# Gate and up stage: a weight load moved to mid block, and row sums moved from the first to the second block of each pair

## The chip, the core and the metric

The kernel runs on one core of a Trainium2 chip. Times are device microseconds (us). The time before is 1020.63 us, the median of three runs (1020.56 to 1021.0). The profile comes from a further execution.

A core has five engines that work side by side, each through its own instructions in order. The profile calls them PE (TensorE, the matrix products; PEld is its loading of the weights), DVE (VectorE), ACT (ScalarE), POOL (GpSimd) and SP (SyncE, which here only issues DMA transfers; its rows read SPq).

## What is computed

The reference mixes two branches of the same input x (2048 rows by 640 columns) with a gate for each row:

```python
g = sigmoid((x * gate_w).sum(-1, keepdims=True))
a = dft_seq_re @ (x @ dft_hid_re.T) - dft_seq_im @ (x @ dft_hid_im.T)
b = (gelu(x @ w_gate) * (x @ w_up)) @ w_down
out = g * a + (1 - g) * b
```

All inputs are float32. w_gate and w_up are 640 by 1728, w_down is 1728 by 640.

## The kernel before, in words

**Products.** Each float32 operand is split into a high part (rounded to the type float32r, on ACT: `high`, line 81) and a low part, the rest (on DVE: `low`, line 84). One product is three matmuls, high by high, high by low and low by high (`mm3`, lines 99 to 103, so PE rows carry the lines L101, L102, L103). Tile names end in h and l for the two parts and in r for the raw data. The products are put together from two by two blocks in a scheme that needs seven block products in place of eight, at the price of sums of blocks on DVE. The names A11, A12, A22, S1 to S4 stand for weight blocks and their sums, T1 to T4 for the sums of the right hand side.

**Stages.** First comes a short stage with the narrow columns, then the gate and up stage (blocks f = 1 to 12, lines 1178 to 1260, some 46 to 334 us of the profile), then the product with w_down, the product along the sequence and the product along the hidden dimension.

**The gate and up stage.** Block f computes 128 columns of x @ w_gate and x @ w_up, for two halves of the rows (tp = 0 and 1), with `gate_up` (line 501). From f = 3 on the blocks come in pairs. `pair_of(f)` gives 1 for the first block of a pair (3, 5, 7, 9, 11, some 30 us each) and 2 for the second (4, 6, 8, 10, 12, some 18 us each). A first block also runs `together` (line 428, banks H, Z, V with the ending t) and `together_up` (line 468, banks with the ending u), which do one product of the pair over both halves of the rows. `together_up` needs weights made from `load_up` (tile wu..r, lines 227 to 232), by `make_up` (line 241: `across`, then the high parts, then `low_u`), and the tiles xu, which POOL loads back from DRAM with `load_across` (line 1148) three times in each first block from f = 5 on. In the same way POOL loads three tiles xq for `together` toward the end of the second block ahead of it.

**What sets the order.** While a block's products are traced, a list `fills` of small pieces of work for the other engines is worked off. Each piece has a cost in ns; `fill` (line 1155) takes pieces from the front as PE's work advances, and never two costless ones in a row after another piece. So a piece's place in `fills` is its place in the program, and `in_order` (line 108) holds PE, ACT, DVE and POOL to the program's order in this stage. SP isn't held: its transfers are placed by the compiler's scheduler, and start when the slot of their tile is free.

The pieces that the change touches:

- `make_w(f + 1)` (line 264) makes the weights of the next block: their sums on DVE, high parts on ACT, low parts on DVE or, in a first block's weights, by a negated copy on ACT and an accumulating transfer on POOL (`left_of`, line 95). Its list is `work`, lines 367 to 378.
- `sum_wd(k)` (line 606) prepares weights of the last product, that with w_down: `load` fetches the tiles dr (512 KB, line 612) and da (128 KB), and two pieces `do` of two DVE sums each (lines 595, 596, 599, 600) form block sums, which SP stores to wsd (line 602). Before, `load` is called at the top of each first block, and the two sums stand behind `make_up`.
- `load_z(n)` (line 709) serves the gate's logits: `load` fetches a tile xz of x (320 KB, line 716), and `total` (line 720) multiplies it by gate_w and adds up each row, on DVE. Sixteen such tiles are needed, ten of them in this stage. Before, two go into each of the blocks 5, 7, 9 and 11, and one into 6 and 8 (`ZE_AT`).

**Slots.** Most tiles, raw, high or low, share 46 equal slots of 4 KB in each partition (`slot`, line 72). A tile that finds none free waits until an earlier tile's last reader is done: the DMA issue or the engine that writes it first waits. Small tiles (da, wb) and half tiles have pools of their own.

Of the kernel before, what the change touches and what calls it, by code (L numbers as in the profile page):

```python
# [22 lines left out]
NF = F // P  # L23
# [4 lines left out]
EORD = [0, 2, 1, 3, 4]  # L28
PAIRED = 3
ZB_AT = [5,7,9,14,15,16]  # L30
ZE_AT = [6, 8]
XB_DOWN = [17, 18]
XB_AT = [1, 3, 4, 5, 9, 10]
WU_AT = [4, 17, 19, 33, 35]
# [3 lines left out]
def kernel(  # L38
# [33 lines left out]
    def slot(dt, shape, name):  # L72
        return pool.tile(shape, dt, tag="s4", name=name, bufs=46)
# [33 lines left out]
    @contextmanager  # L107
    def in_order(*engines):

        traced = nc.cur_bb.bb.instructions  # L110
        mark = traced[-1]
        yield
        start = next(k for k in reversed(range(len(traced))) if traced[k] is mark) + 1
        dep = mybir.DependencyInfo(mybir.DependencyClass.NoSync, mybir.DependencyReason.DATA)
        prev = {}
        for ins in traced[start:]:
            if ins.engine in engines:
                if ins.engine in prev:
                    tc.add_manual_dep(ins, prev[ins.engine].name, dep, reason="in_order")
                prev[ins.engine] = ins  # L120
# [21 lines left out]
    def at(hilo, i):  # L142
        h, l = hilo
        return h[:, i], l[:, i]
# [60 lines left out]
    def pair_of(f):  # L205


        return 0 if f < PAIRED or f >= NF else 2 - (f - PAIRED + 1) % 2
# [18 lines left out]
    def load_up(f):  # L227

        r = slot(F32, [P, 8, P], f"wu{f}r")
        nc.sync.dma_start(r[:, 0:2], wf[f, :, 2:4])  # L230
        nc.sync.dma_start(r[:, 6:8], wf[f - 1, :, 2:4])
        return r
# [8 lines left out]
    def make_up(f, r):  # L241

        W, own = {}, {}

        def across():
            tt(r[:, 2], r[:, 0], r[:, 1], op=ALU.add)
            tt(r[:, 4], r[:, 6], r[:, 0], op=ALU.subtract)
            tt(r[:, 3], r[:, 2], r[:, 6], op=ALU.subtract)
            tt(r[:, 5], r[:, 7], r[:, 3], op=ALU.subtract)

        def high_u():
            own["u"] = [slot(F32R, [P, 8, P], f"wu{f}{n}") for n in "hl"]
            high(own["u"][0][:, 1:6], r[:, 1:6])

        def low_u():
            u = own["u"]
            low(u[0][:, 1:6], u[1][:, 1:6], r[:, 1:6])
            W["A22p"] = at(u, 1)
            for k in range(4):
                W[f"S{k + 1}p"] = at(u, 2 + k)  # L260

        return W, [(112, across), (0, high_u), (78, low_u)]
# [343 lines left out]
    def sum_wd(k):  # L606

        work = []

        def load():  # L610
            r, a21 = slot(F32, [P, 8, P], f"dr{k}"), wsmall(F32, f"da{k}")
            nc.sync.dma_start(r, wd[k, :, :8])
            nc.sync.dma_start(a21, wd[k, :, 8:])
            work.extend(do for _, do in sums_left(nc.sync, r[:, 0:2], r[:, 2:4], r[:, 6:8], a21, wsd[k]))

        def do():
            work.pop(0)()

        return [(0, load), (84, do), (84, do)]
# [89 lines left out]
    def load_z(n):  # L709

        r, work = {}, []

        def load():
            sb = zq.pop(0)
            r[0] = sb, slot(F32, [P, D], f"xz{sb}")
            nc.sync.dma_start(r[0][1], xz[sb])

        def total():
            sb, v = r.pop(0)
            nc.vector.tensor_tensor_reduce(v, v, gwb, 1.0, 0.0, ALU.mult, ALU.add, z[:, sb : sb + 1])  # L720

        return [(0, load), (80, total)] * n
# [99 lines left out]
    def split_pieces(i):  # L822

        n = "{}{}{}".format(*kseq[i])
        r, raw = kraw.pop(i)
        names = ("A11", "A12", "e5", "S4")
        assert not kseq[i][1]
        B, W = [], {}

        def weights():  # L830
            h, l = slot(F32R, [P, 8, P], f"kh{n}"), slot(F32R, [P, 8, P], f"kl{n}")
            split(h, l, r)
            W.update({name: (at((h, l), 2 * q), at((h, l), 2 * q + 1)) for q, name in enumerate(names)})

        def right(q):
            v = hl(f"kb{n}{q}")
            split(*v, raw[q])
            B.extend([at(v, 0), at(v, 1)])

        ktile[i] = W, B  # L840
        return [(122, weights), (122, lambda: right(0)), (122, lambda: right(1))]
# [177 lines left out]
    with in_order(ACT, DVE, PE):  # L1019
# [5 lines left out]
        for d in range(ND):  # L1025
# [20 lines left out]
            if d == 0:  # L1046
                wh, wl = W0["m"][0]
                for c in halves:
                    for k, (w, x) in enumerate(((wh, h), (wl, h), (wh, l))):
                        first = k == 0 and c is halves[0]  # L1050
# [33 lines left out]
        W, work = make_w(1)  # L1084
# [68 lines left out]
    fills, state = deque(), {}  # L1153
# [15 lines left out]
            fill(ns)  # L1169
            next(steps)  # L1170

    s1t, s4 = {}, {}
    Tp.update(B11=at(Bs[0][2, 1], 0), B21=at(Bs[0][2, 1], 1), B22=at(Bs[1][2, 1], 1))
    blocks = [("11", xt[0, 2]), ("12", xt[2, 2]), ("22", xt[2, 3]), ("21", xt[0, 3])]
    keptp, loadp, t123, t4 = sums_across("xp", Tp, blocks, lambda: at(Bs[1][2, 1], 0))
# [2 lines left out]
    with in_order(PE, ACT, DVE, POOL):  # L1178
        for f in range(1, NF):
            kind = pair_of(f)  # L1180
            if f == PAIRED:
                loadu()
                fills.extend([*t4, *u123[:3], *late_work, *u123[3:], *u4])
            fills.extend(todo)
            todo.clear()
            if kind == 1:
                up, work = make_up(f, load_up(f))
                fills.extend(work)
            if kind == 1:
                lw, *w = sum_wd((f - PAIRED) // 2)  # L1190
                lw[1]()
                fills.extend(w)
            if f == PAIRED - 1:
                loadp()
                fills.extend(t123)
            if f == NF - 1:
                lw, *w = sum_wd(NK - 1)
                lw[1]()
                fills.extend(w)
            if f + 1 < NF:  # L1200
                nxt, work = make_w(f + 1)
                if kind != 1 or f == PAIRED:
                    fills.extend(work)
            if kind == 1 and f > PAIRED:
                (_, first), z1, (_, second), z2 = load_z(2)
                first()
                k = len(fills) // 2
                more = list(fills)
                fills.clear()
                fills.extend([*more[:k], z1, (0, second), *more[k:], z2, *work])  # L1210
            elif f in ZE_AT:
                (_, first), z1 = load_z(1)
                first()
                fills.insert(5, z1)
            if f == NF - 1:
                load_k(0)
                fills.extend(split_pieces(0))
                gates(0)
                nc.scalar.activation(table, table, AF.Gelu_apprx_tanh)
            state.update(pe=0, done=0, all=sum(c for c, _ in fills), pe_all=2450 if not kind else 2994 if kind == 1 else 1768)  # L1220
            s5 = pair(F32, f"s5{f}")
            xs = {}
            work = [gate_up(f, W, Bs[tp], tp, s5[:, tp], s1t, xs, s4) for tp in range(2)]
            more = together(f, W, Tp, s1t, xs) if kind == 1 else iter(())
            more_up = together_up(f, W, up, s4) if kind == 1 else iter(())
            store_left()
            if f in LEFT_AT:
                left_work.extend(LEFT_AT[f]())
                if f in (2, 12):
                    k = len(fills) // (2 if f == 2 else 1)  # L1230
                    rest = [fills.pop() for _ in range(len(fills) - k)]
                    fills.extend([*left_work, *reversed(rest)])
                    state["all"] = sum(c for c, _ in fills)
                    left_work.clear()
            for _ in range(4):
                run(more)
            for step in range(8 if not kind else 7):
                for tp, w in enumerate(work):
                    run(w)
                    if (step, tp) in ((0, 1), (1, 1)):  # L1240
                        run(more)
                        if step == 0:
                            run(more)
                    if (2, 0) < (step, tp) < (6, 0):
                        run(more_up)
                if step < 2 and kind == 1 and f > PAIRED:
                    for k in ((1,), (2, 3))[step]:
                        load_across(f, "xu", Tu, keptu, k)
                if step == 4 and pair_of(f + 1) == 1 and f + 1 > PAIRED:
                    for k in (1, 2, 3):  # L1250
                        load_across(f + 1, "xq", Tp, keptp, k)
                if step == 5:
                    load_w(f + 2)
                if f == NF - 1 and step > 4:
                    load_k(step - 4)
            for v in (more, more_up):
                next(v, None)
            while fills:
                fills.popleft()[1]()
            W = nxt  # L1260
# [438 lines left out]
```

## Time and profile before

| | |
|---|---|
| median of three runs | 1020.63 us |
| the profiled execution, in all | 1021.83 us |
| its span, first to last instruction | 1020.0 us |
| instructions | 13269, of them 4483 matmuls |
| DMA | 267.58 MB, mean 262 GB/s |
| mean granted TensorE clock | 1.000 |

How to read the rows that follow. In a timeline a row has the start in us from the span's start, the duration, the engine, the line, the operation, the tile written, `<-` and the tiles read, the shape, and in brackets the idle time of the engine ahead of it with what ended it as inferred. "x2" means two instructions merged into the row. In the rows of windows there follow, after the stretch and its length, the busy us of each engine with its instructions in parentheses in the order PE, PEld, DVE, ACT, POOL, then the granted clock, the DMA engines' busy share and GB/s. Rows of DMA issues end with the count, the size of one and the median us from issue to landing. "DMA to landing" rows give least, median and most for one tile. A matmul's end is modelled and overlaps the next one's start, so distances between starts tell more than durations.

### The profile page before, as it was taken

To read this page: it belongs to the slowest core of one execution; us is meant where nothing else is said; L and a number is where in the kernel's file an instruction comes from. 1 tells how busy PE (TensorE), PEld (TensorE's weight loads), DVE (VectorE), ACT (ScalarE), POOL (GpSimd) and SP (SyncE) were. 2 spreads that over 40 slices of the span, in tenths; PEclk is the share of its full clock that TensorE was granted. 3 is DMA by queue.
4 is the path that set the end of the run, shared out by engine and by line. 5 is a ranking of instruction groups with operands and counts; after the bars stand their busy time and mean duration, and the time that the engine had idled before them with its cause. 6 is when DMAs were issued, how large, how long until landed. Compare 5 with 4: busy or idle time off the path is not lost.

```text
span 1020.0 us, 13269 instructions
## 1 busy us (share of the span) xinstructions
PE 1015.6 (100%) x4483; PEld 840.2 (82%) x4483; DVE 823.2 (81%) x1154; ACT 486.1 (48%) x622; POOL 166.9 (16%) x295
## 2 busy tenths in 40 slices
PE   9999999999999999999999999999999999999998
PEld 7888888888888888888888888888888888888887
DVE  6987877787787989888887976898588869797796
ACT  5544534353535667557444443444344444455440
POOL 0122242323231200100001012102210200021112
PEclk9999999999999999999999999999999999999999
DMA  7468588968699999979874669668866877897856
GB/s 271 168 209 276 181 264 275 314 225 290 201 315 313 415 374 383 330 245 329 295 254 172 213 223 337 223 200 298 302 203 209 294 252 275 295 349 215 274 134 99
DMA packets 96644, 267.58 MB, mean 262 GB/s; under 512 B 12672, under 2 KB 27008, under 8 KB 96576
## 3 DMA queue, kind: packets, MB, share of 16 engines
q1 hardware_dynamic: 70512, 185.24, 53.2%
q0 software_dynamic: 25776, 81.30, 24.4%
q8 instruction: 35, 0.57, 0.2%
q14 instruction: 33, 0.27, 0.1%
q10 hardware_dynamic: 288, 0.20, 0.1%
HBM read 192.48 MB, written 70.27 MB: 258 GB/s over the span
## 4 chain that ended last, share of the span: by engine, by line
PE 97%; issue 1%; DMA 1%; DVE 0%; POOL 0%; POOLq 0%
PE pX L103 6%; PE pX L102 6%; PE pX L101 6%; PE pZ L103 4%; PE pZ L102 4%; PE pZ L101 4%; PE pL L102 3%; PE pL L103 3%; PE pL L101 3%; PE pV L102 2%; PE pV L103 2%; PE pV L101 2%; PE pY L102 1%; PE pR L103 1%; PE pQ L101 1%; PE pQ L102 1%
## 5 line engine op out<-in xcount | busy, mean ns | idle before, releaser
L82 ACT ACTIVATE ch<-csa 128x1024 fp32r<-128x1024 f32 x32 | 34.0, 1063 | 78.2 <-DVE csa L770 76.7
L85 DVE TENSOR_TENSOR cl<-cra,ch 128x1024 fp32r<-128x1024 f32 x32 | 39.1, 1222 | 24.6 <-ACT ch L82 22.5
L82 ACT ACTIVATE ch<-cra 128x1024 fp32r<-128x1024 f32 x32 | 33.9, 1059 | 52.3 <-DVE cl L85 19.3
L85 DVE TENSOR_TENSOR cl<-crb,ch 128x1024 fp32r<-128x1024 f32 x32 | 39.1, 1223 | 14.4 <-ACT ch L82 14.4
L102 PE MATMUL pL<-cl,xah 128*128 128x512 f32 x128 | 49.9, 390 | 0.0
L103 PE MATMUL pL<-ch,xal 128*128 128x512 f32 x128 | 49.9, 390 | 0.0
L101 PE MATMUL pL<-ch,xah 128*128 128x512 f32 x128 | 49.7, 390 | 0.0
L82 ACT ACTIVATE ch<-crb 128x1024 fp32r<-128x1024 f32 x32 | 33.8, 1055 | 31.2 <-PE pL L102 11.4
L404 POOL DMA_DIRECT2D hA<-s x48 | 26.1, 544 | 132.7 <-DVE s L562 113.1
L85 DVE TENSOR_TENSOR cl<-csb,ch 128x1024 fp32r<-128x1024 f32 x32 | 39.2, 1225 | 3.7 <-ACT ch L82 2.3
L85 DVE TENSOR_TENSOR cl<-csa,ch 128x1024 fp32r<-128x1024 f32 x32 | 39.1, 1221 | 2.1 <-ACT ch L82 1.1
L82 ACT ACTIVATE ch<-csb 128x1024 fp32r<-128x1024 f32 x32 | 34.0, 1062 | 11.7 <-DVE csb L773 4.7
L556 ACT ACTIVATE s<-s 128x512 f32<-128x512 f32 x24 | 15.2, 633 | 46.7 <-DVE s L555 46.7
L148 ACT ACTIVATE s<-pX 128x512 f32<-128x512 f32 x40 | 23.5, 598 | 23.7 <-PE pX L103 22.4
L85 DVE TENSOR_TENSOR kl<-kw,kh 128x1024 fp32r<-128x1024 f32 x24 | 29.4, 1223 | 4.5 <-DMA kw<-in_wd 2.6
L82 ACT ACTIVATE kh<-kw 128x1024 fp32r<-128x1024 f32 x24 | 25.3, 1052 | 16.1 <-PE kR L103 6.2
L551 DVE TENSOR_TENSOR s<-s,pX 128x512 f32<-128x512 f32 x24 | 16.5, 686 | 19.6 <-PE pX L103 14.3
L1346 POOL DMA_DIRECT2D uA<-c x8 | 4.3, 542 | 168.9 <-DVE c L1448 168.7
L404 POOL DMA_DIRECT2D hT<-s x48 | 26.0, 541 | 24.3 <-DVE s L579 8.1
L929 POOL DMA_DIRECT2D out<-ks x12 | 6.5, 541 | 136.8 <-DVE ks L928 136.2
L101 PEld LDWEIGHTS pL<-ch,xah 128*128 128x128 f32 x128 | 24.0, 188 | 5.0
L102 PEld LDWEIGHTS pL<-cl,xah 128*128 128x128 f32 x128 | 24.0, 188 | 5.0
(3612 smaller groups left out, 3483.8 us busy)
## 6 DMA issues: line engine op xcount, KB each, us to landing
cra<-in_ct SPq DMA_DIRECT2D x64, 512.0 KB, 4.6
crb<-in_ct SPq DMA_DIRECT2D x64, 512.0 KB, 5.0
hA<-s POOLq DMA_DIRECT2D x48, 256.0 KB, 5.9
hT<-s POOLq DMA_DIRECT2D x48, 256.0 KB, 5.7
kr<-hA SPq DMA_DIRECT2D x24, 512.0 KB, 7.7
kr<-hT SPq DMA_DIRECT2D x24, 512.0 KB, 6.8
ux<-uA SPq DMA_DIRECT2D x24, 512.0 KB, 5.9
ux<-uT SPq DMA_DIRECT2D x16, 512.0 KB, 6.7
```

Source lines behind the costliest of these rows:

```text
L82: nc.scalar.activation(hi, raw, AF.Copy)
L85: nc.vector.tensor_tensor(lo, raw, hi.bitcast(F32), op=ALU.subtract)
L101: nc.tensor.matmul(ps, lh, rh, start=first, stop=False, skip_group_check=True)
L102: nc.tensor.matmul(ps, lh, rl, start=False, stop=False, skip_group_check=True)
L103: nc.tensor.matmul(ps, ll, rh, start=False, stop=last, skip_group_check=True)
L148: nc.scalar.activation(m, src, AF.Copy)
L404: nc.gpsimd.dma_start(to[:, i], src)
L551: tt(s5, s5, X, op=ALU.add)
L556: nc.scalar.activation(s2, s2, AF.Gelu_apprx_tanh)
L929: nc.gpsimd.dma_start(acc4[:, t] if tp and e == 4 else out[2 * tp + t, e], src)
L1346: nc.gpsimd.dma_start(to[:, i], src)
```

## The change

Three things move, all in the loop of the gate and up stage:

1. In the first blocks from f = 5 on, `load` of `sum_wd` (`lw`) becomes a piece of `fills` behind the three pieces of `make_up`, ahead of the pieces of the next block's weights. The two DVE sums go behind the fifth of those pieces, the low parts of the next block's A weights. Block 3 keeps its order.
2. No piece of `load_z` stands in first blocks any longer, except that the blocks 7 and 9 fetch one tile as their last piece; its row sum is kept in `zlate` and goes into the next block, at position 4 of its list.
3. The second blocks 4, 6, 8 and 10 fetch two tiles each at their top, with the row sums at positions 9 and 12 of the list.

So the row sums lie 2, 2, 3, 3 in the blocks 4, 6, 8, 10, where they lay 2, 1, 2, 1, 2, 2 in 5, 6, 7, 8, 9, 11.

```diff
-ZE_AT = [6, 8]
+ZE_AT = (7, 9)
...
-    s1t, s4 = {}, {}
+    s1t, s4, zlate = {}, {}, []
...
             if kind == 1:
                 lw, *w = sum_wd((f - PAIRED) // 2)
-                lw[1]()
-                fills.extend(w)
+                if f == PAIRED:
+                    lw[1]()
+                    fills.extend(w)
...
             if kind == 1 and f > PAIRED:
-                (_, first), z1, (_, second), z2 = load_z(2)
-                first()
-                k = len(fills) // 2
-                more = list(fills)
-                fills.clear()
-                fills.extend([*more[:k], z1, (0, second), *more[k:], z2, *work])
-            elif f in ZE_AT:
-                (_, first), z1 = load_z(1)
-                first()
-                fills.insert(5, z1)
+                fills.extend([lw, *work[:5], *w, *work[5:]])
+                if f in ZE_AT:
+                    fetch, z1 = load_z(1)
+                    fills.append(fetch)
+                    zlate.append(z1)
+            elif kind == 2 and f < NF - 1:
+                if zlate:
+                    fills.insert(4, zlate.pop())
+                for k in (9, 12):
+                    (_, do), z1 = load_z(1)
+                    do()
+                    fills.insert(k, z1)
```

## The prediction, made before the changed kernel ran

> **What bounds the kernel now.** I read the page's busy table first, then the span (1020.0 us) cut into five stretches, of which three are shown.
>
> ```profile
> PE 1015.6 (100%) x4483; PEld 840.2 (82%) x4483; DVE 823.2 (81%) x1154; ACT 486.1 (48%) x622; POOL 166.9 (16%) x295
> ```
> ```profile
> 20.00:200.00 180.00, 180.00 (x794) 148.82 (x794) 146.36 (x246) 84.12 (x131) 45.77 (x82) 1.00 0.70 233
> 200.00:220.00 20.00, 19.88 (x88) 15.97 (x87) 13.97 (x29) 8.73 (x15) 2.47 (x5) 1.00 0.81 275
> 220.00:1000.00 780.00, 780.00 (x3442) 646.22 (x3441) 638.37 (x840) 379.34 (x452) 114.99 (x201) 1.00 0.80 272
> ```
>
> TensorE is busy for the whole span, at granted clock 1.00. A busy PE hides short gaps, because a matmul's shown time (0.39 us) is longer than the distance to the next one; so I count starts. From 220 to 1000 there are 3442 matmuls in 780 us, 226.6 ns each; from 20 to 200, 794 in 180 us, 226.7 ns each. That is one pitch throughout. Only 200:220 falls below its full length (19.88), and its PEld share is lower too (15.97 in 20 us, against 148.82 in 180 us, which is 16.54 in 20). The one gap lies here, in the timeline of PE and the chain of waits:
>
> ```profile
> 212.50 0.39 PE L103 MATMUL pX<-xT03h,ws7l 128*128 128x512 f32 x1
> 213.01 0.50 PE L101 MATMUL pH7u<-xu,wu7h 128*128 128x512 f32 x1
> 213.34 0.40 PE L102 MATMUL pH7u<-xu,wu7h 128*128 128x512 f32 x1
> ```
> ```profile
> 207.69 5.28 DMA xu<-xv
> ```
>
> The three starts are 0.51 and 0.33 us apart where 0.227 is the pitch: 0.28 + 0.10, and 0.01 in the next, **0.39 us lost**, in block 7 of the gate and up stage. PE waited for xu (the second tile of the block's up sums), whose load POOL issued at 207.69. Why so late, VectorE, POOL and SP tell:
>
> ```profile
> 197.88 0.68 DVE L585 TENSOR_TENSOR s<-s,s 128x512 f32<-128x512 f32 x1
> 202.20 0.83 DVE L720 CUSTOM_DVE_ANT_0 xz<-xz,gwb 128x640 f32<-128x640 f32 x1 [3.64 <-DMA hT<-s]
> ...
> 206.46 0.82 DVE L85 TENSOR_TENSOR wu7l<-wu7r,wu7h 128x640 fp32r<-128x640 f32 x1 [0.57 <-DMA hT<-s]
> ...
> 208.57 0.42 DVE L600 TENSOR_TENSOR dr<-dr 128x256 f32<-128x256 f32 x1
> ```
> ```profile
> 202.58 0.55 POOL L1150 DMA_DIRECT2D xu<-xv  x1 [0.30 <-issue]
> 207.69 1.14 POOL L1150 DMA_DIRECT2D xu<-xv  x2 [4.56 <-DVE dr L595]
> ```
> ```profile
> 191.04 0.62 SPq L612 DMA_DIRECT2D dr<-in_wd  x1
> 192.44 0.33 SPq L716 DMA_DIRECT2D xz<-in_xz  x1
> ```
> ```profile
> DMA to landing us min/median/max: 8.7/9.2/9.6
> ```
> ```profile
> xu<-xv POOLq DMA_DIRECT2D x12, 512.0 KB, 5.6
> xz<-in_xz SPq DMA_DIRECT2D x10, 320.0 KB, 7.8
> dr<-in_wd SPq DMA_DIRECT2D x5, 512.0 KB, 7.2
> ```
>
> (The three transfers are from the DMA list of this stage, 95 to 340: KB each, median us to landing.) VectorE stood 3.64 us at the logits' product L720. The wait's row names an hT store, but L720 reads only xz and gwb; the row of landings (8.7/9.2/9.6) is that of block 7's two xz tiles, and a load issued at 192.44 that takes 9.6 us lands at 202.0, just ahead of L720; so I read it as the xz landing. Behind it in VectorE's order stand the up-weights' sums and wu7l, the last reader of wu7r. POOL's xu loads start 0.41 us after wu7l ends (207.28), which fits a wait for wu7r's slot; the row blames the instruction behind it, L595.
>
> **The change part by part.** No instruction is added or dropped: ten L720 products, ten xz loads and the same dr loads, placed elsewhere. The matmuls stay 4483 at the same pitch, so the time can change only by PE's gaps, and 0.39 us is all that can be won after the first 20 us.
>
> *The logits' products leave the first blocks* (5, 7, 9, 11: two each before, none after). In block 7 VectorE gets back 3.64 + some 0.8 = 4.4 us ahead of wu7l, since its work before L720 ends at 198.6 (L585). So wu7l should end near 207.3 - 4.4 = 202.9, and the xu loads, two issues from about 203.3 on (behind the block's first xu load at 202.6), should land by 203.9 + 5.6 = 209.5. PE wants them at 212.73 (212.50 plus one pitch). **The 0.39 us go**, and 3 us are to spare. What is late next in that block is dr, below.
>
> *They enter the second blocks* (two in 4 and 6, three in 8 and 10). Against before that is +2, +1, +2, +3 products of 0.8 us: 1.6, 0.8, 1.6 and 2.4 us on VectorE. The cover is the idle time of VectorE ahead of the first product S3 or of wd in each of these blocks:
>
> ```profile
> 136.98 0.29 DVE L85 TENSOR_TENSOR wd<-wb,wd 128x128 fp32r<-128x128 f32 x1 [3.31 <-ACT wd L82]
> ...
> 185.68 0.69 DVE L551 TENSOR_TENSOR s<-s,pX 128x512 f32<-128x512 f32 x1 [1.65 <-ACT s L547]
> ...
> 233.81 0.69 DVE L551 TENSOR_TENSOR s<-s,pX 128x512 f32<-128x512 f32 x1 [3.58 <-ACT s L547]
> ...
> 280.47 0.29 DVE L85 TENSOR_TENSOR wd<-wb,wd 128x128 fp32r<-128x128 f32 x1 [3.31 <-ACT wd L82]
> ```
>
> 3.31, 1.65, 3.58 and 3.31 us cover 1.6, 0.8, 1.6 and 2.4: cost 0. Without that cover each would cost its own length at most, 6.4 us together. One product is not covered: in blocks 8 and 10 the one fetched in the block before goes in ahead of the second sums across (position 4), so wq, its accumulate on POOL and the xq load behind it slide by 0.8 us.
>
> ```profile
> 283.43 1.24 POOL L1150 DMA_DIRECT2D xq<-xp  x2 [3.35 <-DMA wq11l<-wq11r]
> ```
> ```profile
> 290.08 0.39 PE L101 MATMUL pH11t<-xq,wq11h 128*128 128x512 f32 x1
> ```
> ```profile
> DMA to landing us min/median/max: 4.1/4.9/6.7
> ```
>
> The last row is for the three xq of block 10. There 283.43 + 0.8 + 4.9 = 289.1, 1.0 us ahead of PE; at the longest landing 290.9, 0.8 late. For block 8 I take the same bounds: 0 and 1.6 us together. I take 0, the median of the landings being the row that fits the two tiles in question.
>
> *The xz loads move with them.* Two are issued at the top of each second block, a third at the end of blocks 7 and 9 behind dr and its stores on SP. They leave a stretch (190 to 205) in which block 7's first half had dr, xz and the hA and hT stores at once. The landing of 7.8 us must now fit between the block's top and the positions 9 and 12 of its list; see the second rival.
>
> *dr is loaded behind wu's low parts* instead of at the block's top, its two sums go behind low_a of the next block's weights. VectorE now waits for dr, with both S3 sums (L551), the next sums' low parts (low_c), L490 and both S4 sums (L555) queued behind, and PE waits for L490. If dr is issued only when wu7r's slot comes free, at 202.9, it lands at 210.1; its four sums take 1.7 us (from wu7l's end at 207.28 to L600's at 208.99), so they end at 211.8. The first S3 product behind them ends only at 212.9 (its last matmul, 212.50 + 0.39): cost 0, by 1.1 us. If SP gets an older slot, it is earlier still.
>
> The Trainium skill, "DMA: Bandwidth & Descriptors", section "Rules for kernel authors", says the opposite of this edit: issue the transfer early, compute, wait late. The same page's section "Anatomy of one DMA" gives 2.0 us plus bytes over 436 GB/s, an estimate of 3.2 us for dr's 512 KB. By that figure dr would land at 206.1 and no cost could arise; the row (7.2 us) says otherwise, and the sum goes by the row.
>
> **Sum.** 1020.0 of span - 0.4 = 1019.6 for the profiled execution. That execution took 1021.83 us in all, 1.20 above the median of the three runs; so I subtract the 0.4 from the median: 1020.63 - 0.39 = **1020.2 us**.
>
> **The rivals.** *It doesn't do what it says.* The xu loads wait for some other slot than wu7r's and stay late, or the gap stays at 0.2 to 0.6 us: 1020.4 to 1020.8, say 1020.6. For it speaks that the slot's owner is only inferred; against it, that the timing fits wu7l to 0.41 us. Chance 0.12.
>
> *The late xq* (above): 1020.2 + 0 to 1.6, up to 1021.8. Chance 0.09.
>
> *Slower: dr's slot passes on late.* Now the high parts of block 8's sums wait for dr's four stores, in the slot that dr leaves:
>
> ```profile
> 215.09 1.06 ACT L82 ACTIVATE ws8h<-ws8r 128x1024 fp32r<-128x1024 f32 x1 [0.48 <-DMA wsd<-dr]
> ```
> ```profile
> 217.32 0.68 DVE L490 TENSOR_TENSOR s<-s,pH7u 128x512 f32<-128x512 f32 x1
> ```
> ```profile
> 219.26 0.39 PE L101 MATMUL pH7u<-xT14h,wu7h 128*128 128x512 f32 x1
> ```
>
> From ws8h's start to the end of L490 it is 2.9 us (218.0 - 215.09), and pH7u would be due at 218.87 without the 0.39. The release came 6.1 us after the last sum (209.0 to 215.1). With the sums ending at 211.8 it comes at 217.9, L490 ends at 220.8, and PE loses 1.9 us, in each of blocks 5, 7, 9, 11 where the slots fall that way: 1022.1 with one, 1028 with four. It decides once the last sum ends after 218.87 - 2.9 - 6.1 = 209.9, that is, if dr lands after 208.2. For it speaks that the forecast's own dr lands at 210.1 when it takes wu7r's slot. Against it: the first half of the block holds two xz tiles less, so older slots are free for ws8h, or for dr itself. Chance 0.13. This is where the rule of the Trainium skill on issuing early would come out right.
>
> *Slower: the third xz lands late.* In blocks 8 and 10 three tiles need slots. In block 8 the first S3 sum must end by the first row's start:
>
> ```profile
> 237.62 0.39 PE L101 MATMUL pX<-x05h,wa 128*128 128x512 f32 x1
> ```
> ```profile
> 226.02 0.54 POOL L404 DMA_DIRECT2D hT<-s  x1 [0.18 <-issue]
> ```
> ```profile
> hT<-s POOLq DMA_DIRECT2D x48, 256.0 KB, 5.7
> ```
>
> L720, the sum behind it and S3's take 0.8 + 0.2 + 0.7, so the tile must land by 235.9 and be issued by 228.1. Slots of block 7's weights come free with its last matmuls, some 2 us behind 219.26, which is in time. If the tile got that of s, freed by the last hT store of that block (226.02 + 5.7 = 231.7), it would land at 239.5: 3.6 us in each of two blocks, 1027. Chance 0.07.
>
> **How the numbers follow.** The forecast, 1020.2, has 0.58; its own spread is that of the three runs, 1020.0 to 1020.8. 0.2% is 2.04 us, about what a measurement of this kernel can tell from no change. Faster by that is five times the gap that the starts show: 0.01. The two slower rivals hold 0.20, of which some 0.02 (one block alone) stays within 2 us: slower 0.18, within 0.2% either way 0.81. The range goes from 1019.8 to 1022.6, through the late xq and the dr rival in one block, and leaves out about 0.17.
>
> **What would show it.** Right: no L720 between 190 and 221, wu7l ending near 203, the second xu load issued near 203, every PE start of block 7 0.227 apart, xq ahead of 290.08 in block 10. Wrong: PE gaps at the last pH.u of the blocks 5, 7, 9, 11 with ws.h released by a wsd store; gaps at the last pX of block 8 or 10 with VectorE waiting at L720; or PE starts off the pitch in the later stages, which this change should not touch.

## The result, and the profile after

The changed kernel takes 1022.53 us (median of 20 executions, 1021.55 to 1029.86), the kernel before, on the same chip, 1021.05 us (20 executions, 1020.45 to 1022.62). The ratio is 1.0022, with a 95% interval of 1.0014 to 1.0030: 1.5 us slower, where 0.4 us faster was forecast. Of the 2.3 us between the forecast of 1020.2 and the result, 0.4 lie in the kernel before, whose median was 1020.63 in three executions and 1021.05 in twenty. The profiled execution took 1022.97 us with a span of 1021.2 us, 1.2 us more than that of before.

The stretches 20 to 200, 200 to 220 and 220 to 1000 again, now of the changed kernel:

```profile
20.00:200.00 180.00, 180.00 (x794) 148.74 (x794) 148.04 (x253) 84.70 (x131) 46.47 (x83) 1.00 0.71 235
200.00:220.00 20.00, 20.00 (x90) 16.49 (x89) 11.56 (x21) 9.76 (x16) 1.86 (x4) 1.00 0.71 236
220.00:1000.00 780.00, 778.45 (x3434) 644.32 (x3433) 637.76 (x840) 379.42 (x452) 114.58 (x200) 1.00 0.80 272
```

Two things are to be seen. 200:220 is full (20.00 with 90 matmuls, 88 before): the gap of block 7 is gone. And 220:1000, full before with 3442 matmuls, now lacks 1.55 us and holds 3434, eight matmuls fewer. The waits of PE name the place, and the timeline of PE shows it:

```profile
PE pH11t L101 <- DMA xq<-xp: 1.6, 1, 1.6
```
```profile
285.98 0.39 PE L101 MATMUL pH11t<-x021h,wa11h 128*128 128x512 f32 x1
...
289.15 0.39 PE L103 MATMUL pV11t<-x05h,wa11l 128*128 128x512 f32 x1
291.09 0.50 PE L101 MATMUL pH11t<-xq,wq11h 128*128 128x512 f32 x1 [1.55 <-DMA xq<-xp]
291.43 0.39 PE L102 MATMUL pH11t<-xq,wq11h 128*128 128x512 f32 x1
```

The starts are 1.94 and 0.34 us apart where 0.227 is the pitch: 1.71 + 0.11 = 1.8 us lost in block 11, on the second of the three xq tiles. Won 0.4, lost 1.8. How xq became late stands in the rows of VectorE, ACT and POOL in block 10 of the changed kernel:

```profile
273.73 0.68 DVE L525 TENSOR_TENSOR s<-s,pX 128x512 f32<-128x512 f32 x1
274.33 0.82 DVE L720 CUSTOM_DVE_ANT_0 xz<-xz,gwb 128x640 f32<-128x640 f32 x1
275.08 0.08 DVE L720 DVE_READ_ACCUMULATOR2_ANT z<- 128x1 f32 x1
275.08 0.28 DVE L291 TENSOR_TENSOR wq11r<-wa11r,wq11r 128x128 f32<-128x128 f32 x1
```
```profile
275.60 0.96 ACT L82 ACTIVATE wq11h<-wq11r 128x896 fp32r<-128x896 f32 x1 [1.74 <-DVE wq11r L292]
```
```profile
278.31 0.86 POOL L97 DMA_DIRECT2D wq11l<-wq11r  x1 [3.67 <-DMA wa11l<-wa11r]
279.13 0.60 POOL L1150 DMA_DIRECT2D xq<-xp  x1
284.95 0.56 POOL L1150 DMA_DIRECT2D xq<-xp  x1 [5.22 <-DMA wq11l<-wq11r]
```

The kept row sum (274.33 to 275.08) stands ahead of L291 and L292, and ACT waits for L292; wq's accumulating transfer follows, and the second xq load waits for that transfer to land, which frees wq11r's slot (by the row's releaser). The rows of the kernel before for the accumulate and for the first matmul of block 11:

```profile
278.24 0.86 POOL L97 DMA_DIRECT2D wq11l<-wq11r  x1 [2.92 <-ACT wq11l L93]
```
```profile
286.66 0.39 PE L101 MATMUL pH11t<-x021h,wa11h 128*128 128x512 f32 x1
```

Measured from that matmul (285.98 in the changed kernel, 286.66 before), the accumulate is issued 7.67 us ahead (8.42 before): the 0.75 us of the row sum. The changed kernel's row names the landing of wa11l as what ended POOL's wait. That is a coincidence: in two kernels below, e3_z_only and e8_wa_behind, wa11l lands later (7.49 and 7.40 us ahead) and the accumulate is still issued 7.67 us ahead, and in all four it follows the end of ACT's negated copy (L93) by 0.4 us. The second xq is issued 1.03 us ahead (3.23 before): 2.2 us later. These rows give the difference, first the landing of wq11l, then that of the second xq:

```profile
DMA to landing us min/median/max: 6.2/6.2/6.2
```
```profile
DMA to landing us min/median/max: 6.1/6.1/6.1
```

Before, the same two rows read 4.8 and 4.1. So a slip of 0.75 us grew by 1.4 us in the first landing and by 2.0 in the second: 4.2 us in all. The tile landed 5.07 us behind the block's start in place of 0.87, and PE wants it at 3.40.

The same slip in block 8 cost nothing. There the accumulate was issued 7.67 us ahead of block 9 too, landed in 4.6 us (4.1 before), and the second xq was issued 2.66 us ahead (3.92 before), landed in 3.6 us and was 2.5 us in time.

### The profile page after: what moved, and what is told of

Its sections match the earlier page's. It is cut to its first block, busy times and chain, and to the rows that moved or that the text cites. A ratio compares the mean times of both kernels' runs of the same rounds, so it can differ in the third digit from the quotient of the medians.

```text
span 1021.2 us, 13283 instructions
## 1 busy us (share of the span) xinstructions
PE 1015.3 (99%) x4483; PEld 840.0 (82%) x4483; DVE 823.3 (81%) x1154; ACT 487.7 (48%) x622; POOL 167.2 (16%) x295
## 4 chain that ended last, share of the span: by engine, by line
PE 94%; issue 3%; DMA 1%; POOL 1%; DVE 0%; POOLq 0%
PE pX L101 6%; PE pX L103 6%; PE pX L102 6%; PE pZ L101 4%; PE pZ L103 4%; PE pZ L102 4%; PE pL L103 3%; PE pL L101 3%; PE pL L102 3%; PE pV L103 2%; PE pV L101 2%; PE pV L102 2%; PE pY L103 1%; PE pR L103 1%; PE pQ L103 1%
## 5 line engine op out<-in xcount | busy, mean ns | idle before, releaser
L537 ACT ACTIVATE s<-pZ 128x512 f32<-128x512 f32 x24 | 14.2, 595 | 30.2 <-PE pZ L103 29.2
```

The costliest lines, as they stand in the source:

```text
L537: nc.scalar.activation(s5, Z, AF.Copy)
```

## The experiments

**Theory A**: VectorE's 0.75 us ahead of the second sums across does it, by way of wq's accumulate and crowded transfers. **Rival B**: the third xz tile of the blocks 8 and 10 crowds the transfers. **Rival C**: what costs is dr's later load. All twelve are read in one table. The first two columns are PE's loss by starts: from the first matmul of block 7 to that of block 9 beyond 47.68 us, and from the first of block 11 to PE's last beyond 729.52 us (the distances in profiles without a gap). The 0.45 of before are the prediction's 0.39 and small excesses in the matmuls behind. The last two belong to the second xq for block 11, measured from that block's first matmul: issue, and landing (wanted at 3.40; landings are read to 0.1 us).

| kernel | block 7 | block 11 on | median us (n) | ratio, 95% | issue | landing |
|---|---|---|---|---|---|---|
| before | 0.45 | 0.0 | 1021.05 (20) | | -3.23 | 0.87 |
| changed | 0.0 | 1.87 | 1022.53 (20) | 1.0014 to 1.0030 | -1.03 | 5.07 |
| e1_late5 | 0.0 | 0.0 | 1021.00 (11) | 0.9991 to 1.0009 | -3.23 | 1.67 |
| e2_no_third | 0.99 | 0.0 | 1021.42 (11) | 0.9999 to 1.0016 | -3.24 | 0.96 |
| e3_z_only | 0.0 | 0.0 | 1022.21 (11) | 1.0004 to 1.0023 | -1.78 | 2.92 |
| e4_dr_only | 1.87 | 0.0 | 1021.82 (11) | 1.0001 to 1.0019 | -3.23 | 1.87 |
| e5_before_delay | 0.05 | 0.12 | 1022.32 (11) | 0.9999 to 1.0016 | -1.76 | 3.34 |
| e6_after_delay2 | 0.60 | 0.34 | 1022.81 (12) | 1.0012 to 1.0034 | -5.80 | 1.60 |
| e7_late5_z | 0.0 | 0.0 | 1020.93 (12) | 0.9992 to 1.0011 | -3.21 | 1.99 |
| e8_wa_behind | 0.0 | 1.56 | 1021.99 (11) | 0.9996 to 1.0013 | -1.58 | 2.02 |
| e9_after_again | 0.75 | 0.94 | 1022.17 (1) | | -1.14 | 3.96 |
| e10_wa12_behind | 1.94 | 1.82 | 1022.91 (12) | 1.0002 to 1.0024 | -1.30 | 2.80 |
| e11_dr_not5 | 0.0 | 0.0 | 1021.13 (11) | 0.9991 to 1.0008 | -3.23 | 0.77 |
| e12_z_behind_up | 1.79 | 0.0 | 1021.91 (12) | 1.0000 to 1.0021 | -3.22 | 2.08 |

The ratios are to the kernel before, run on the same chip with each set: 1021.1 with e1 to e4, 1021.3 with e5 to e8, 1021.16 with e9 to e11, 1021.26 with e12.

### The first set: which part of the change

e1_late5 puts the kept row sum one place later, behind the second sums across:

```diff
-                    fills.insert(4, zlate.pop())
+                    fills.insert(5, zlate.pop())
```

> The kept row sum of blocks 8 and 10 goes one place further back, behind the second sums across; all else as changed. Theory A (the 0.75 us that VectorE adds ahead of the second sums across push wq's accumulate into the first xq load and the second xq load behind wa12r): PE's gap in block 11 (1.7 us) goes, time 1.2 to 1.8 us under the changed kernel, 1020.2 to 1020.8. Theory B (three xz tiles in a second block crowd the DMA engines and the slots, wherever VectorE uses them): the gap stays at 1.3 us or more. Theory C (dr loaded later is what costs): no difference from the changed kernel.

e2_no_third fetches no third tile; the two row sums it leaves over go into the last stretch of blocks, as elsewhere in the kernel:

```diff
-ZE_AT = (7, 9)
-ZB_AT = [5,7,9,14,15,16]
+ZE_AT = ()
+ZB_AT = [5, 7, 9, 11, 13, 14, 15, 16]
```

> Blocks 7 and 9 fetch no xz tile, so blocks 8 and 10 have two each; the two tiles left over are done in the product with w_down, at its steps 11 and 13. Theories A and B: the gap in block 11 goes, 1020.2 to 1020.8 unless the two steps of the later stage lose something of their own. Theory C: it stays, 1022 to 1022.6.

e3_z_only moves the row sums alone, e4_dr_only dr alone (in the first blocks from 5 on). Both edits are shown against the changed kernel, cut to what matters:

```diff
-                if f == PAIRED:
-                    lw[1]()
-                    fills.extend(w)
+                lw[1]()
+                fills.extend(w)
...
-                fills.extend([lw, *work[:5], *w, *work[5:]])
+                fills.extend(work)
```
```diff
-ZE_AT = (7, 9)
+ZE_AT = [6, 8]
...
-                fills.extend([lw, *work[:5], *w, *work[5:]])
...
+                (_, first), z1, (_, second), z2 = load_z(2)
+                first()
+                more = list(fills)
+                fills.clear()
+                fills.extend([*more[:4], z1, (0, second), *more[4:], lw, z2, *work[:5], *w, *work[5:]])
```

> The xz tiles and their row sums are placed as in the changed kernel, dr is loaded at the block's top with its sums behind the up-weights, as before. Theories A and B: the gap in block 11 stays (1 to 2 us), time 1021.5 to 1022.6. Theory C: no gap, 1020.2 to 1020.8.

> dr is loaded mid block and its sums stand behind low_a as in the changed kernel, the xz tiles and their row sums stand where they stood before. Theories A and B: no gap in block 11; the 0.4 us in block 7 may stay, since the row sum again waits ahead of wu7l: 1020.4 to 1021.0. Theory C: 1.7 us in block 11 or the like elsewhere, 1022 to 1022.6.

One place later is all it takes: 1021.0 us, no gap, three tiles as in the changed kernel. B falls with that. e1_late5 also has dr moved in every block as the changed kernel has it, so C alone does not explain the changed kernel's loss. e2_no_third, which B and A both allow, loses nothing in block 11, as A needs, but 0.99 us in block 7, so its time (1021.42) missed the forecast. The POOL rows of e1_late5 carry it:

```profile
277.51 0.86 POOL L97 DMA_DIRECT2D wq11l<-wq11r  x1 [2.92 <-DVE ws11r L282]
279.20 0.56 POOL L1150 DMA_DIRECT2D xq<-xp  x1 [0.83 <-DVE wb L296]
282.69 0.55 POOL L1150 DMA_DIRECT2D xq<-xp  x1 [2.93 <-DMA wq11l<-wq11r]
```

Its first xq load is issued 1.69 us behind the accumulate, where the changed kernel has 0.82, and the accumulate lands in 4.8 us again. Over all fourteen profiles the landing of wq11l goes with that distance: 4.8 us in the seven where it is 1.27 us or more, 5.5 to 6.2 in the seven where it is 0.93 or less. That two numbers go together is no test of the cause; none was made for this step. The seven with the short distance are also the seven in which the accumulate itself is issued late (7.07 to 7.69 us ahead), and for block 7 the accumulate lands in 5.4 to 6.9 us in ten profiles in which the first xq follows only 3.8 us or more behind it: other transfers stretch it too. e3_z_only has the accumulate as late as the changed kernel (7.67 us ahead); in its profiled execution, the fastest of eleven, the tile landed 0.5 us in time, so that the forecast gap is not seen, yet the median is 1022.21: the row sums alone cost about 1.1 us.

e4_dr_only was the surprise: dr alone costs too, at another place, while the row sums stay in the first blocks. PE there, then the SP rows of the same kernel in block 5:

```profile
193.13 0.39 PE L103 MATMUL pV7t<-x05h,wa7l 128*128 128x512 f32 x1
195.10 0.50 PE L101 MATMUL pH7t<-xq,wq7h 128*128 128x512 f32 x1 [1.58 <-DMA xq<-xp]
```
```profile
163.41 0.33 SPq L602 DMA_DIRECT2D wsd<-dr  x1
163.87 0.34 SPq L602 DMA_DIRECT2D wsd<-da  x1
164.33 0.88 SPq L602 DMA_DIRECT2D wsd<-dr  x2
168.39 0.33 SPq L218 DMA_DIRECT2D wa7r<-in_wf  x1
```

It is again the second xq, now that for block 7. Block 5's dr stores come later and wa7r's load with them (168.39, 163.81 before).

### The second set: the delay by itself, doubled, and the landing

e5_before_delay puts an operation of the same length, without any transfer, into the kernel before; e6_after_delay2 puts the same one into the changed kernel, beside the kept row sum:

```diff
+            if f in (8, 10):
+                fills.insert(4, (80, lambda: tt(gwb, gwb, gwb, op=ALU.max)))
```

> The kernel before, with one added VectorE instruction in each of the blocks 8 and 10: a maximum of gwb with itself (128x640, about 0.75 us, changes nothing), at the place where the changed kernel has its kept row sum, ahead of the second sums across. No row sum, xz load or dr load moves. Theory A (VectorE's time ahead of the second sums across is the cause, whatever it computes): wq's accumulate is issued 0.75 us later, the second xq load for block 11 goes from 3.23 us ahead of the block's start to between 1 and 2.5 us ahead, lands 0.5 us ahead to 1.7 us late, and the time is 0.5 to 1.5 us over before (1021.6 to 1022.6) when before is 1021.1. Theory B (the three xz tiles of blocks 8 and 10 crowd the transfers): same as before, 1020.9 to 1021.3, with the second xq landing at least 2 us ahead of its use. Theory C (dr loaded later): same as before.

> The changed kernel with the same added maximum of gwb with itself (0.75 us) beside the kept row sum in blocks 8 and 10, so that twice the time stands ahead of the second sums across. Theory A: wq's accumulate 0.75 us later again (6.9 us ahead of the start of block 11 where the changed kernel has 7.7), the second xq load 0.8 to 1.5 us later than there; PE's gap in block 11 grows from 1.7 to 2.5 to 3.2 us, a gap of up to 1 us opens in block 9 (there the load lands 2.5 us ahead in the changed kernel), and the time is 0.8 to 2.5 us over the changed kernel's 1022.5 (1023.3 to 1025). If long gaps lower the granted clock, more executions show 0.996 to 0.998 and the time goes over that. Theories B and C: within 0.4 us of the changed kernel.

e7_late5_z is e3_z_only with the kept row sum at position 5.

> Row sums as in the changed kernel but the kept one at position 5 (behind the second sums across), and dr's load and sums left where the kernel before has them. Theory A: wq's accumulate and the second xq loads keep the places of before (3.2 us ahead in block 11), block 7's gap of 0.39 us at pH7u is gone, no other gap: 0.3 to 0.4 us under before, 1020.6 to 1020.8 when before is 1021.1. Theory B: three tiles in blocks 8 and 10 still cost, 1021.5 or more. Theory C says nothing against A here: it gives the same 1020.7.

e8_wa_behind gives three loads, which SP issues within a microsecond of the second xq, to POOL behind the xq loads:

```diff
-        nc.sync.dma_start(ra, wf[f - 1, :, :8])
+        (nc.gpsimd if f == 12 else nc.sync).dma_start(ra, wf[f - 1, :, :8])
...
-        nc.sync.dma_start(r[:, 0:2], wf[f, :, 2:4])
-        nc.sync.dma_start(r[:, 6:8], wf[f - 1, :, 2:4])
+        (nc.gpsimd if f == 11 else nc.sync).dma_start(r[:, 0:2], wf[f, :, 2:4])
+        (nc.gpsimd if f == 11 else nc.sync).dma_start(r[:, 6:8], wf[f - 1, :, 2:4])
```

> The changed kernel; the load of wa12r and the two of wu11r are issued by POOL, in its order behind the three xq loads (wu11r behind four hA stores too), where SP issues them in the changed kernel at the moment at which POOL issues the second xq load. All other engines keep their instructions and order. It tells whether the length of the second xq's landing (6.1 us there, 4.1 to 4.9 in the kernel before) comes from sharing the DMA engines with wa12r and wu11r. If so (A with the collision): the second xq load is issued 1.0 us ahead of block 11's start as in the changed kernel, but lands in 4.1 to 5 us, and PE's gap in block 11 is 0 to 0.7 us in place of 1.7; time 1021.2 to 1022. If not (the landing is long for the hA stores and the third xq load behind it): 5.5 to 6.2 us of landing, gap of 1.2 to 1.8, time 1022.2 to 1022.8.

e5: 0.75 us of VectorE and nothing else moves the second xq from 3.23 to 1.76 us ahead and its landing from 0.87 to 3.34, which is 0.06 us in time in the profiled execution (its fastest, 1021.12). The median of 1022.32 lies 1.0 over before, but the interval of the ratio begins at 0.9999: the issue and the landing are shown, the time only leans that way.

e6 missed: the gap in block 11 did not grow. The POOL rows say why:

```profile
279.47 0.86 POOL L97 DMA_DIRECT2D wq11l<-wq11r  x1 [4.53 <-ACT wq11l L93]
280.10 1.35 POOL L1150 DMA_DIRECT2D xq<-xp  x2
285.90 0.56 POOL L1150 DMA_DIRECT2D xq<-xp  x1 [4.45 <-DMA wq11l<-wq11r]
```

The first two loads now go out together and the third waits for the accumulate. With a changed program the tiles took other slots, and the xq load that waits for wq11r's is now the one whose tile PE wants 3.4 us later. (That the slots changed is inferred from the releasers in these rows.) What is left are gaps of 0.2 to 0.3 us in several blocks, 1.5 us in all, of which the table leaves out 0.57 between the starts of the blocks 9 and 11. So the price of the delay seems to hang on which tile stands in that slot.

e7 came out near its forecast (1020.93 where 1020.6 to 1020.8 was expected): the second xq for block 11 is issued 3.21 us ahead as before, no gap is left in either block, and B, which expected 1021.5 or more, fails once more.

e8 was right on the landing, which is even shorter than the 4.1 to 5 us expected; the load was also issued 1.58 us ahead, not 1.0. The rows are SP's in the changed kernel, then POOL's in e8_wa_behind with the landing of the load at 284.42:

```profile
284.59 0.33 SPq L218 DMA_DIRECT2D wa12r<-in_wf  x1
285.02 0.37 SPq L230 DMA_DIRECT2D wu11r<-in_wf  x1
285.44 0.42 SPq L231 DMA_DIRECT2D wu11r<-in_wf  x1
```
```profile
284.42 0.55 POOL L1150 DMA_DIRECT2D xq<-xp  x1 [4.61 <-DMA wq11l<-wq11r]
285.19 0.56 POOL L1150 DMA_DIRECT2D xq<-xp  x1 [0.22 <-issue]
285.86 0.54 POOL L218 DMA_DIRECT2D wa12r<-in_wf  x1
```
```profile
DMA to landing us min/median/max: 3.6/3.6/3.6
```

3.6 us in place of 6.1, and no gap at xq. But wu11r behind four stores came so late that xu was, at the end of the block:

```profile
309.24 0.50 PE L101 MATMUL pH11u<-xu,wu11h 128*128 128x512 f32 x1 [1.24 <-DMA xu<-xv]
```

### The third set: the changed kernel again, and block 7

> The changed kernel itself, a second profiled execution. Theory A: wq's accumulate and the first xq load for block 11 stand 7.67 and 6.85 us ahead of the block's start as in the first one, since VectorE's order sets them; only the landings differ, so that the second xq is issued 1.0 to 1.8 us ahead and PE's gap is between 0 and 1.8 us. From the start of block 11 to PE's last matmul it is 729.5 us plus that gap. If the gap were a chance of that one execution, the accumulate would stand near 8.4 us ahead and no landing would exceed 5 us.

e10_wa12_behind keeps only the first line of e8's edit; e11_dr_not5 is e4_dr_only with block 5 as before (its edit against e4_dr_only):

```diff
-                if f == PAIRED:
+                if f in (PAIRED, 5):
...
-                fills.extend([*more[:4], z1, (0, second), *more[4:], lw, z2, *work[:5], *w, *work[5:]])
+                if f == 5:
+                    k = len(more) // 2
+                    fills.extend([*more[:k], z1, (0, second), *more[k:], z2, *work])
+                else:
+                    fills.extend([*more[:4], z1, (0, second), *more[4:], lw, z2, *work[:5], *w, *work[5:]])
```

> The changed kernel; only the load of wa12r goes to POOL, behind the three xq loads; wu11r's two loads stay with SP. If wa12r is what stretches the second xq's landing: it lands in 3.6 to 4.6 us, no gap over 0.5 us in block 11 and, wu11r being as early as in the changed kernel, none at pH11u either: 1021.0 to 1021.5 when before is 1021.2. If wu11r does it: landing 5.5 to 6.2, gap 1 to 1.8 us, 1022.2 to 1022.8.

> As the kernel that only loads dr later and leaves the row sums where the kernel before has them (1021.82, with a gap of 1.7 us in block 7), but with block 5's dr, its sums and row sums as in the kernel before; dr moves in the blocks 7, 9 and 11 alone. If it is block 5's later dr that shifts block 6's transfers (wa7r was issued 4.6 us later there, its accumulate landed in 7.2 in place of 5.9): wq7l lands in 4.2 to 4.9 us, the second xq for block 7 is ahead by over 1 us, no gap in block 7, 1020.8 to 1021.3. If it is what is loaded in block 7 itself (two xz tiles at 190 without dr): landing of that xq over 6 us again, gap of 0.8 to 1.7, 1021.6 to 1022.1.

e9, the changed kernel again, has the accumulate at the same 7.67 us ahead and a smaller gap in block 11 (0.94 by starts), and it shows a second gap, of 0.75 us, in block 7, on the second xq for that block. e10 supports the collision: with wa12r alone moved the load lands in 4.1 us and no gap at xq is left in block 11. That makes two profiles with wa12r close (6.1 and 5.1 us) against two without (3.6 and 4.1). Its time was missed all the same (1022.91): 1.94 us went in block 7, where nothing of this edit stands, and 1.8 us from block 11 on, in small gaps of later stages. These losses come and go: four of its 12 executions took 1020.1 to 1020.6 us. e11 answers for dr: with block 5 left alone, wa7r's load is back at 163.62, the second xq for block 7 is issued 3.86 us ahead and lands 2.5 us in time, and the median is 1021.13, with all eleven executions between 1020.66 and 1021.63. So, with the row sums left where they were, dr's move is free in the blocks 7, 9 and 11, and not in block 5.

### The last: one row sum, and nothing else

e12_z_behind_up tests the prediction's first step alone, in the kernel before:

```diff
-                k = len(fills) // 2
+                k = 5 if f == 7 else len(fills) // 2
```

> The kernel before with one edit: in block 7 the first row sum stands behind the sums across of the up-weights, just ahead of their low part. No transfer moves to another block, no other row sum and no dr. If the late xz is what keeps wu7l late (the prediction's first step) and nothing else of the change is needed: VectorE waits for xz ahead of wu7l only until some 202, wu7l ends near 203.7 in place of 207.3, the 0.39 us at pH7u go, the second xq loads keep the places of before (3.2 to 3.9 us ahead of blocks 7, 9, 11), so that no gap is left from 20 us to the end of the stage: 0.4 us under before, which the times of this kernel can hardly tell from none (ratio 0.9990 to 1.0003), and clearly under the changed kernel's 1022.5.

It failed, and shows how a wait moves. VectorE, ACT and PE of e12_z_behind_up in block 7:

```profile
205.68 0.82 DVE L85 TENSOR_TENSOR wu7l<-wu7r,wu7h 128x640 fp32r<-128x640 f32 x1 [4.47 <-ACT wu7h L82]
...
211.04 0.82 DVE L720 CUSTOM_DVE_ANT_0 xz<-xz,gwb 128x640 f32<-128x640 f32 x1 [2.83 <-DMA xz<-in_xz]
```
```profile
204.91 0.74 ACT L82 ACTIVATE wu7h<-wu7r 128x640 fp32r<-128x640 f32 x1 [1.28 <-DMA hT<-s]
...
212.79 0.63 ACT L82 ACTIVATE wa<-wa8r 128x512 fp32r<-128x512 f32 x1 [3.82 <-DVE wa8r L309]
...
214.80 0.60 ACT L148 ACTIVATE s<-pH7u 128x512 f32<-128x512 f32 x1
```
```profile
215.44 0.50 PE L101 MATMUL pH7u<-xu,wu7h 128*128 128x512 f32 x1 [1.50 <-ACT s L148]
```

The first row sum waits no more, but wu7l now waits for wu7h, which ACT starts only at 204.91, behind two evictions of pZ (201.03 and 203.03), and the block's second row sum waits 2.83 us for its tile. L309 and ACT's work on wa8r stand behind it, and the eviction of pH7u behind those (214.80), for which PE waits by its row. The loss in block 7 grew from 0.45 to 1.79 us. So this place does not close the gap. Two other kernels show that the row sums need not leave block 7 for it. e11_dr_not5 keeps both and only takes dr's load from the top of the block:

```profile
198.50 0.82 DVE L720 CUSTOM_DVE_ANT_0 xz<-xz,gwb 128x640 f32<-128x640 f32 x1
...
202.10 0.82 DVE L85 TENSOR_TENSOR wu7l<-wu7r,wu7h 128x640 fp32r<-128x640 f32 x1
```

The first xz tile lands there in 6.5 us (9.6 before), L720 waits for nothing, wu7l ends at 202.9 and block 7 loses nothing. And e5_before_delay, whose block 7 has the program of the kernel before, lost 0.05 us there and not 0.45, with that tile landing in 8.3 us: the gap that the prediction set out to win is not in every execution.

No kernel here is measurably faster than before. The shortest median is that of e7_late5_z, 1020.93 beside 1021.3, and its interval holds 1.

## Why the prediction was wrong, point by point

**The gap of block 7: right.** In the changed kernel's first profile wu7l ends at 201.98 (203 forecast), the next xu load is issued 0.4 us behind, and the matmuls of pH7u stand at the pitch. That no more than 0.4 us was to be won was right too. The late xz was the right link, as e11_dr_not5 and e5_before_delay bear out: with the tile earlier, the gap goes without any row sum moved. But the 0.4 us rested on one execution.

**Row sums at positions 9 and 12: right.** VectorE's idle time covers them; e1_late5 and e7_late5_z have them all and lose nothing. What their loads do to other transfers is told below.

**dr inside its block: right.** The rows of VectorE in block 7 of the changed kernel:

```profile
209.43 0.42 DVE L595 TENSOR_TENSOR dr<-da,dr 128x256 f32<-128x256 f32 x1 [2.49 <-DMA dr<-in_wd]
...
210.81 0.43 DVE L600 TENSOR_TENSOR dr<-dr 128x256 f32<-128x256 f32 x1
212.66 0.69 DVE L551 TENSOR_TENSOR s<-s,pX 128x512 f32<-128x512 f32 x1 [1.43 <-PE pX L103]
```

dr lands at 209.2 (210.1 forecast), the sums end at 211.2 (211.8), and VectorE then waits 1.43 us for PE. The load took 5.3 us, between the 7.2 that the sum used and the 3.2 that the prediction worked out from the figure of the Trainium skill ("DMA: Bandwidth & Descriptors", section "Anatomy of one DMA"). That figure is a fit for transfers issued by GpSimd, and SP issues dr. ws8h starts at 213.84 without waiting for a store: the rival on dr's slot did not come, nor did the one on the third xz (no L720 of the blocks 8 and 10 has idle time ahead of it).

**The late xq: the step that failed.** The prediction named the place, the chain and the slide, and priced it at 0 to 0.8 us for each block, taken at 0 (chance of more: 0.09). The slide of wq's accumulate was as forecast (0.75 us). The failure is that it added this slide to landings of the old profile, 4.9 and at longest 6.7, as if the second xq load moved by the same 0.75 us. Its release is the landing of another transfer, and that landing grew by 1.4 us, in step with the first xq load coming closer behind it (argued, not tested); its own grew by 2.0 us (1.0 in e9) as it met wa12r, which e8 and e10 support. 0.75 + 1.4 + 2.0 make 4.15 of the 4.20 us measured, against a margin of 2.5 (0.87 to 3.40). The price was 1.87 us where 0.8 was the bound. In block 9, where the second xq was issued 1.3 us ahead of the next block's weight load (wa10r) and not behind it, the price was 0 as forecast.

**Forgotten altogether: dr's later stores in block 5.** The step on dr followed what is queued behind the sums on VectorE and who waits for the stores' slots, both inside the same block. It did not follow SP into block 6. e4 and e11 show that this alone, with the row sums left in place, costs 1.87 us in block 7, in one profile, and 0.7 us in the median. There the rule on issuing early, which the prediction quoted from the Trainium skill ("DMA: Bandwidth & Descriptors", section "Rules for kernel authors"), was the right warning, for a reason that lies one block later. It does not explain the changed kernel's loss: e1_late5 moves dr in the same way and loses nothing, and in the changed kernel's first profile wa7r is issued at 163.30, no later than before (163.81). In e9 it is late too (166.31), but e1_late5 has it still later (167.55) without a gap.

**Forgotten too: the second xz tile in block 6.** Of its two profiles one shows the changed kernel losing 0 and 1.87 us in the blocks 7 and 11, the other 0.75 and 0.94. The loss in block 7 is on the second xq for that block, wanted 3.40 us behind its start. It landed at 1.2 us before, and at -0.1 to 0.9 in e5, e11 and e12. In all nine profiles of kernels whose block 6 fetches two xz tiles it landed at 2.0 to 5.2 us, also in e3_z_only (2.2) and e7_late5_z (2.6), which leave dr alone. (e4, with one tile there, has 5.1 by its late wa7r.) So the row sums' move takes a good part of block 7's margin without costing a gap in most profiles. That it does so by the second xz load is argued from what goes together, not tested, and which transfers stretch the landing of wq7l ahead of it is open (4.5 us before, 5.4 and 6.2 in the changed kernel, 5.8 and 6.1 in e3 and e7, 5.9 in e4). How the losses share out in the 20 executions that were only timed is open as well.

## What to carry to other kernels

When an edit delays a transfer, do not add the delay to the old landing: look up which transfers it now meets, and treat the landing as a range that the delay itself widens. Follow a chain of transfers to its last user by margins (here 2.5 us from landing to use), and give a step that eats a third of the margin a real chance of eating all of it. And a list of small pieces has places that are not alike: one place earlier or later decided here whether a covered 0.75 us was free. Last, a gap of 0.4 us in one profile may be missing in the next execution of the same code, as block 7's was in e5_before_delay.

## What the runs showed of the hardware

A transfer here seems to land later where another engine's load is issued just ahead of it. The second xq load for block 11, 512 KB, landed in 6.1 and 5.1 us with wa12r (512 KB) issued by SP 0.36 and 0.25 us ahead of it (the changed kernel twice), in 4.7 and 5.1 us with wa12r 0.4 us behind it (e3, e5), and in 3.6 and 4.1 us with wa12r behind it on POOL (e8, e10). Issued 1.8 us ahead of wa12r, it took 4.0 to 5.3 us in seven kernels, so only the 6.1 stands clear of that spread. The Trainium skill, "DMA: Bandwidth & Descriptors", section "Queues, rings and completion order", says that each of the 16 engines takes packets in turn from the queues for which it has work; these landings fit that, though no profile here was read packet by packet.

A lower granted clock leaned toward kernels with gaps, and no more than that. Of 108 executions of the kernel before beside the experiments none shows a mean clock of 0.998 or less. Of kernels with a gap of over 0.5 us in some profile, 4 of 20 of the changed kernel do (1025.78 to 1029.86 us), 4 of 12 of e10, 2 of 12 of e12, 1 of 11 of e2, and none of 11 of e4 and of e8; e6, with small gaps, has 2 of 12, e5 none of 11. Of the kernels without a gap in their profile, e3 has 1 of 11, e7 1 of 12, e1 and e11 none of 22. No such execution was profiled, so whether a gap lowers the clock is open.
